# Batch 0's scores in six units instead of seven, and more turns by DMA, in a block-sparse attention and feed-forward kernel

## The chip, the cores and the metric

One core of one Trainium2 chip. The metric is the device time of one execution in microseconds (us). Where a time is given as a median, the lowest and highest run stand beside it at its first mention. The profile's span is about 1.7 us shorter than the time of the same run.

Engines by the profile's names: PE is TensorE, DVE is VectorE, ACT is ScalarE, POOL is GpSimd, SP is SyncE, whose queue issues the DMAs.

## The reference

Attention over 4 batches of 8 heads, 768 positions and 64 dimensions, then a feed-forward layer on the 3072 tokens. A query sees its own block of 64 keys and the three blocks that its gate scores highest, and no later key.

```python
k_rep = k.reshape(B, H, 12, 64, 64).mean(axis=3)            # one mean key per block
gate  = einsum('bhsd,bhnd->bhsn', q, k_rep)                 # later blocks set to -1e9
mask  = top-3 blocks of gate, plus the own block, and key position <= query position
attn  = softmax(where(mask, q @ k.T / 8, -1e9)) @ v
x     = attn.transpose(0, 2, 1, 3).reshape(3072, 512)
out   = gelu_tanh(x @ w_in) @ w_out                         # 512 -> 2048 -> 512
```

## The kernel before

Two heads make a "pair"; pair p belongs to batch p // 4 (HP = 4). Each batch passes three stages: its heads (four pairs), the first layer with gelu ("s1"), and the second layer ("s2"). A list scheduler in Python (`Plan.solve`) is given each piece of work with its engines, an assumed cost, its dependencies, a priority and, for a DMA, a `lag` until it lands. It fixes the order of every engine when the kernel is built; on the chip each engine works through its list and waits where an operand is late. Second-layer matmuls of the batch ahead fill PE where the heads leave room, and 110 filler matmuls on zeros of the lowest priority fill what planned gaps are left. Fillers that find no gap come at the end.

The block mask is a matrix of 12 rows per head. It is computed with queries on the partitions, turned, and added to the scores by a matmul. The normalised output `xn` must be turned too, to be the first layer's operand `xT`. The kernel has two ways for both: six (or five) PE transposes with a copy out of PSUM, or one transposing DMA from the SP queue.

```python
def by_xbar(p):                       # mask rows turned by DMA?
    return p >= 2 * HP
# ... in pre(p), the work ahead of a pair
if by_xbar(p):
    go = add({SP: 1.0}, mask_dma, [sel], pr - 20)          # dma_start_transpose
    m = add({"NONE": 0.0}, lambda _: None, [go], pr, lag=3.0)
else:
    m = add({PE: 0.31}, mask, [sel], pr, takes=("mk", ("mk", p)))
mcs = [add({DVE: 0.4, ACT: 0.6}, mc(h), [m, old.get("s")], pr)
       for h in ((None,) if early else (0, 1))]
# ... in turn(p, norms), the output of a pair of batches 1 to 3
if p >= HP + 2 and hp < HP - 1:
    go = add({SP: 1.0}, ot_dma, norms, base - 20)          # dma_start_transpose
    ...
    return
ot = add({PE: 0.36}, ot_e, norms, base + 50, takes=("pre", ("oT", p)))
```

Batch 0 is special: there is no second layer to fill PE with. Its pairs take both heads in one unit of scores. A unit holds a wide PSUM tile (two exist) from its score matmuls until its exp has read it; POOL then clears the upper triangle of a diagonal tile, and PE multiplies with the values.

```python
units = [[(0, 0, 384)], [(1, 128, 256), (2, 256, 128)], [(0, 384, 384)],   # (key tile, first query, width)
         [(1, 384, 384)], [(2, 384, 384)], [(3, 384, 384)],
         [(4, 512, 256), (5, 640, 128)]]
def both_heads(p):
    for ui, pieces in enumerate(units):
        st = add({PE: 0.45}, st_e, ..., takes=("wide", ("st",) + u))       # scores, then mask
        ex = add({ACT: 0.71}, ex_e, [st, ...], gives=[("st",) + u])        # exp, 128 x 768
        af = add({POOL: 0.36}, af_e, [ex], pr)                             # diagonal tiles only
        pvs.append(add({PE: 0.212}, pv_e, [af, ld["v16", p], ...]))        # times values
        # after units 1 and 6: DVE normalises a half, PE turns it
```

Loads, and the fillers:

```python
ld[key, p] = add({"NONE": 0.0}, lambda _: None, [go], prio=1000 * b + hp, lag=1.9)
...
def warm():
    for n in range(110):
        def emit(_, n=n):
            nc.tensor.matmul(plan.buf["warm", n][:, 0:256], zero, z, start=True, stop=True)
        add({PE: 0.107 if n > 26 else 0.214}, emit, [], 1e6, takes=("warm", ("warm", n)), gives=[("warm", n)])
```

Lines of the kernel that the profile names: L850 batch 0's scores, L868 their exp, L900 their value matmuls, L934 batch 0's output transposes, L977 those of later batches, L521 gates, L567 mask transposes, L587 mask turns by DMA, L984 output turns by DMA, L1018 first layer, L1031 gelu, L1052 second layer, L1089 fillers, L224 and L234 loads. From L850 on, the changed kernel has each one line later (L851, L869 and so on).

The softmax here doesn't subtract the row's maximum and nothing guards it: scores larger than these inputs give would overflow.

Of the kernel before, what the change touches and what calls it, by code (L numbers as in the profile page):

```python
# [9 lines left out]
FP16 = mybir.dt.float16  # L10
# [23 lines left out]
class Plan:  # L34
# [13 lines left out]
    def add(self, *a, **kw):  # L48
        op = Op(*a, **kw)
        self.ops.append(op)  # L50
        return op
# [70 lines left out]
def kernel(  # L122
# [16 lines left out]
    HP = H // 2  # L139
# [11 lines left out]
    iov = ctx.enter_context(tc.tile_pool(name="iov", bufs=PV))  # L151
    hd = ctx.enter_context(tc.tile_pool(name="hd", bufs=3))
    hd2 = ctx.enter_context(tc.tile_pool(name="hd2", bufs=2))
    atp = ctx.enter_context(tc.tile_pool(name="atp", bufs=7))
    xtp = ctx.enter_context(tc.tile_pool(name="xtp", bufs=2))
    gtp = ctx.enter_context(tc.tile_pool(name="gtp", bufs=2))
    obp = ctx.enter_context(tc.tile_pool(name="obp", bufs=3))
# [35 lines left out]
    PE, ACT, DVE, POOL, SP = "PE", "ACT", "DVE", "POOL", "SP"  # L193
    add = plan.add
    T = {}
# [10 lines left out]
        return p >= FIRST_DVE  # L206

    def by_xbar(p):
        return p >= 2 * HP


    SRC = {"k": k, "q": q, "v": v}
# [154 lines left out]
    rdy = {}  # L367
# [381 lines left out]
    def heads(p):  # L749
        b, hp = divmod(p, HP)  # L750
        i = p % NB
        base = 1000 * b + 100 * hp
        norms = []
        for h in range(2):
            pvs = []
            for gi, (ja, jb) in enumerate(groups):
                u = (p, h, gi)
                pr = base + 10 * (3 * h + gi)
                wa = S - ja * 128
                wb = S - jb * 128  # L760

                def st_e(_, u=u, ja=ja, jb=jb, wa=wa, wb=wb, h=h):
                    st = plan.buf[("st",) + u]
                    for jc, cb in ((ja, 0), (jb, wa)):
                        s0 = jc * 128
                        w = S - s0
                        x = cb
                        while x < cb + w:
                            e = min(cb + w, (x // 512 + 1) * 512)
                            k0, q0 = slice(s0, s0 + 128), slice(  # L770
                                s0 + (x - cb), s0 + (e - cb))
                            nc.tensor.matmul(  # L772
                                st[:, x:e], kT16[i][h][0:76, k0],
                                qT16[i][h][0:76, q0],
                                start=True, stop=True)
                            x = e
                st = add({PE: 0.381}, st_e, rdy[p][h], pr,
                         takes=("wide", ("st",) + u))

                def ex_e(_, u=u, n=wa + wb):  # L780
                    T["at", u] = atp.tile([128, 896], FP16, tag="at",
                                          name="at_%d_%d_%d" % u)
                    nc.scalar.activation(
                        out=T["at", u][:, 0:n],
                        in_=plan.buf[("st",) + u][:, 0:n],
                        func=AF.Exp, bias=0.0, scale=SCALE)
                ex = add({ACT: 0.8}, ex_e,
                         [st, table(("exp", b), gelus.get(b - 1, []), base)],
                         pr,
                         gives=[("st",) + u])  # L790
                exps.setdefault(b, []).append(ex)

                def af_e(_, u=u, wa=wa):
                    at = T["at", u]
                    dg = bass.AP(at.tensor, at.offset,
                                 [at.ap[0], [wa, 2], [1, 128]])
                    nc.gpsimd.affine_select(
                        out=dg, in_=dg, compare_op=ALU.is_ge, fill=0.0,
                        base=0, pattern=[[0, 2], [1, 128]],
                        channel_multiplier=-1)  # L800
                af = add({POOL: 0.36}, af_e, [ex], pr)

                def pv_e(_, u=u, ja=ja, jb=jb, wa=wa, h=h, gi=gi):
                    pvv = plan.buf["pv", p, h][:, 0:NC * 66].rearrange(
                        "p (c w) -> p c w", w=66)
                    at = T["at", u]
                    for jc, cb in ((ja, 0), (jb, wa)):
                        for qc in range(jc, NC):
                            nc.tensor.matmul(
                                pvv[:, qc, 0:65],  # L810
                                at[:, cb + (qc - jc) * 128:
                                   cb + (qc - jc + 1) * 128],
                                v16[i][:, jc, h, :],
                                start=(gi == 0 and jc == 0 and qc == 0),
                                stop=(gi == 2 and jc == jb and qc == NC - 1),
                                skip_group_check=True)
                pvs.append(add({PE: 0.212}, pv_e,
                               [af, ld["v16", p], c_E["ones", i]] + pvs[-1:],
                               pr, takes=("pv", ("pv", p, h))))

            norms.append(norm(p, h, pvs, base - 20))
        turn(p, norms)
        last.setdefault(p, {}).update({"s": st, "k": st, "v": pvs[-1]})


    units = [[(0, 0, 384)], [(1, 128, 256), (2, 256, 128)], [(0, 384, 384)],
             [(1, 384, 384)], [(2, 384, 384)], [(3, 384, 384)],
             [(4, 512, 256), (5, 640, 128)]]

    def both_heads(p):  # L830

        b, hp = divmod(p, HP)
# [3 lines left out]
        pvs = []  # L836
        for ui, pieces in enumerate(units):
            u = (p, ui)
            pr = base + 10 * ui

            def st_e(_, u=u, pieces=pieces):

                st = plan.buf[("st",) + u]
                for mask in range(2):
                    x = 0
                    for j, q0, w in pieces:
# [8 lines left out]
                                start=x == 0 and not mask, stop=bool(mask),  # L855
                                skip_group_check=True)
                        x += w
            st = add({PE: 0.45}, st_e, rdy[p][0 if ui < 2 else 1], pr,
                     takes=("wide", ("st",) + u))

            def both(t, lo, hi):
                return t[:, 0:768].rearrange("p (h w) -> p h w", h=2)[
                    :, :, lo:hi]

            def ex_e(_, u=u):
                T["at", u] = atp.tile([128, 896], FP16, tag="at",
                                      name="at_%d_%d" % u)
                nc.scalar.activation(  # L868
                    out=both(T["at", u], 0, 384),  # L869
                    in_=plan.buf[("st",) + u].rearrange(  # L870
                        "p (h w) -> p h w", h=2)[:, :, 0:384],
                    func=AF.Exp, bias=0.0, scale=SCALE)
            ex = add({ACT: 0.71}, ex_e,
                     [st, table(("exp", b), [], base)], pr,
                     gives=[("st",) + u])
            exps.setdefault(b, []).append(ex)
# [1 line left out]
            for n, (j, q0, w) in enumerate(pieces):  # L878
                if q0 != 128 * j:
                    continue  # L880
                x = sum(w for _, _, w in pieces[:n])

                def af_e(_, u=u, x=x):
                    dg = both(T["at", u], x, x + 128)
                    nc.gpsimd.affine_select(
                        out=dg, in_=dg, compare_op=ALU.is_ge, fill=0.0,
                        base=0, pattern=[[0, 2], [1, 128]],
                        channel_multiplier=-1)
                af = add({POOL: 0.36}, af_e, [ex], pr)

            half = 0 if ui < 2 else 1

            def pv_e(_, u=u, ui=ui, pieces=pieces, half=half):
                pvv = plan.buf["pv", p, half][:, 0:NC * 66].rearrange(
                    "p (h c w) -> p h c w", h=2, w=66)
                x = 0
                for j, q0, w in pieces:
                    for c in range(q0 // 128, (q0 + w) // 128):
                        for h in range(2):
                            nc.tensor.matmul(  # L900
                                pvv[:, h, c - 3 * half, 0:65],
                                both(T["at", u], x, x + 128)[:, h],
                                v16[i][:, j, h, :],
                                start=(ui in (0, 2) and x == 0 and h == 0),
                                stop=(ui in (1, len(units) - 1)
                                      and x == 256 and h == 1),
                                skip_group_check=True)
                        x += 128
            pvs.append(add({PE: 0.212}, pv_e,
                           [af, ld["v16", p], c_E["ones", i]] + pvs[-1:],  # L910
                           pr, takes=("pv", ("pv", p, half))))
            if ui == 1 or ui == len(units) - 1:
# [56 lines left out]
    def turn(p, norms):  # L969

        b, hp = divmod(p, HP)
# [13 lines left out]
                out=T["xT", b][:, hp, :].rearrange("p (c q) -> p c q", q=128),  # L985
                in_=T["xn", p].rearrange("p c h d -> p (c h d)"))

        if p >= HP + 2 and hp < HP - 1:
            go = add({SP: 1.0}, ot_dma, norms, base - 20)
            xts.setdefault(b, []).append(  # L990
                add({"NONE": 0.0}, lambda _: None, [go], base - 20,
                    lag=3.0))
            return
# [171 lines left out]
```

## Time and profile before

| | before |
|---|---|
| time | 275.11 us (275.07 to 275.27, 3 runs) |
| span of the profiled run | 273.8 us (that run took 275.51 us) |
| PE busy | 97% |
| first scores of batch 0 / last value matmul of batch 0 | 12.59 / 45.06 us |
| first scores of batch 1, 2, 3 | 66.64 / 132.56 / 193.15 us |

The page of the kernel before: the span, busy time of each engine, and the chain of work that ended last by engine.

```profile
span 273.8 us, 5919 instructions
PE 265.1 (97%) x2290; PEld 153.7 (56%) x2290; DVE 142.2 (52%) x468; ACT 187.4 (68%) x245; POOL 48.5 (18%) x112
PE 63%; DVE 12%; SPq 9%; DMA 6%; ACT 5%; issue 3%; POOL 0%; DVEq 0%; ACTq 0%
```

PE is busy for 97% of the span, but that counts the fillers. The mean hides stages with different limits. What PE waited for in the kernel before (in total, times, longest, in us):

```profile
PE bank_90 L977 <- DVE xn_1329 L964: 1.1, 1, 1.1
PE wide_89 L850 <- ACT at_0_468 L868: 0.8, 1, 0.8
PE bank_92 L977 <- DVE xn_2574 L964: 0.7, 1, 0.7
...
PE bank_90 L521 <- DVE ksb_108 L472: 0.4, 1, 0.4
PE bank_93 L521 <- DVE qT_6_1289 L422: 0.4, 1, 0.4
PE bank_93 L567 <- DVE madd_132 L548: 0.4, 1, 0.4
```

Apart from waits in the first 12 us, that is most of PE's idle time: 1.06 us before the output transposes of pair 4, 0.75 us before scores of batch 0 (for an exp on ScalarE), 0.70 us before the output transposes of pair 11, some 0.4 us before gates and mask transposes. Most are waits for VectorE. The busy time of each engine by window, in the kernel before (columns: window, its length, then busy us and instructions of PE, PE's weight loads, DVE, ACT, POOL, then clock, DMA share, GB/s), two windows of batch 0's heads:

```profile
20.00:28.00 8.00, 6.65 (x96) 3.74 (x94) 7.28 (x28) 5.94 (x9) 1.84 (x5) 1.00 0.89 132
28.00:36.00 8.00, 8.00 (x121) 4.66 (x121) 7.83 (x28) 7.32 (x11) 4.39 (x9) 1.00 1.07 156
```

and two of batch 1's heads:

```profile
70.00:86.00 16.00, 14.18 (x159) 8.19 (x157) 14.47 (x37) 14.52 (x19) 4.07 (x10) 1.00 0.79 143
86.00:102.00 16.00, 15.78 (x181) 8.96 (x180) 15.50 (x51) 15.21 (x19) 6.17 (x14) 1.00 1.00 161
```

In batch 1's heads VectorE is busy for 14.47 and 15.50 us of 16 while PE is the engine that should be the limit. PE's long waits for it, 0.40, 0.37 and 1.06 us, lie in the first of the two windows; in the second PE is idle for 0.22 us only. In batch 0's heads, from 28 us on, VectorE is at 7.83 of 8 and ScalarE at 7.32.

The durations of the exp in batch 0, from ScalarE's timeline of the kernel before (start, us, instruction):

```profile
36.69 0.81 ACT L868 ACTIVATE at_0_815<-wide_89 128x768 f16<-128x768 f32 x1
37.39 0.80 ACT L868 ACTIVATE at_1_830<-wide_88 128x768 f16<-128x768 f32 x1
```

And VectorE's timeline of the kernel before around the values of pair 3, the load that batch 0 uses last, and the queries of pair 4, the first pair of batch 1. A bracket at the end of such a line would give idle time just before it and what ended it; there is none:

```profile
31.73 0.55 DVE L203 CAST v_137<-v_sd_610 128x768 f16<-128x768 f32 x1
...
34.52 0.97 DVE L422 STREAM_TRANSPOSE qT_4_777<-q_sd_650 128x768 f32<-128x768 f32 x1
```

The 1.06 us wait ends with `xn_1329`, pair 4's output normalised on VectorE. It stood there behind work for pair 7 and a copy of mask rows:

```profile
79.08 0.96 DVE L422 STREAM_TRANSPOSE kT_7_1390<-k_sd_1261 128x768 f32<-128x768 f32 x1
80.42 0.48 DVE L203 COPY qT_0_127<-bank_93 12x640 f16<-12x640 f16 x1 [0.38 <-ACT qT_1_128 L199]
...
82.81 0.56 DVE L964 TENSOR_TENSOR xn_1329<-bank_90,zr_1_1436 128x384 f16<-128x384 f32 x1
```

### The profile page before, as it was taken

What the parts mean: (1) busy time and instruction counts of PE and PEld (TensorE: products, weight loads), DVE (VectorE), ACT (ScalarE), POOL (GpSimd) and SP (SyncE); (2) the same over time, 40 slices, a digit from 0 to 9 for tenths busy, and PEclk for the clock granted to TensorE, in tenths of its full rate; (3) what the DMA queues carried; (4) which work ended last, traced back from release to release, by engine and by line L of the source; (5) the groups of instructions that cost most, each with busy time, mean ns of one, the idle gap of its engine ahead of it and who ended that gap; (6) DMA issues with size and microseconds to landing.
All of it is one profiled execution on the core that took longest, in us unless ns stands there. A gap on an engine that the chain in (4) does not pass through costs nothing.

```text
span 273.8 us, 5919 instructions
## 1 busy us (share of the span) xinstructions
PE 265.1 (97%) x2290; PEld 153.7 (56%) x2290; DVE 142.2 (52%) x468; ACT 187.4 (68%) x245; POOL 48.5 (18%) x112
## 2 busy tenths in 40 slices
PE   8798999999998999999999989999999999999998
PEld 5664557665454554455566534565566545665447
DVE  6778997107899996857499968500133300000001
ACT  3477887757989994896999853766899713654110
POOL 5041633000122420000045500000154200000000
PEclk9999999999999999999999999999999999999999
DMA  5999999999889969989999963300022122000222
GB/s 127 229 186 138 139 203 189 190 186 152 123 161 166 156 132 195 220 128 176 163 178 173 148 132 102 86 2 0 0 69 63 36 79 77 0 2 0 77 77 79
DMA packets 133824, 32.44 MB, mean 118 GB/s; under 512 B 127524, under 2 KB 129828, under 8 KB 133796
## 3 DMA queue, kind: packets, MB, share of 16 engines
q1 hardware_dynamic: 130676, 27.87, 58.9%
q0 software_dynamic: 3120, 4.19, 9.2%
q8 instruction: 18, 0.29, 0.5%
q14 instruction: 10, 0.08, 0.1%
HBM read 27.26 MB, written 6.29 MB: 123 GB/s over the span
## 4 chain that ended last, share of the span: by engine, by line
PE 63%; DVE 12%; SPq 9%; DMA 6%; ACT 5%; issue 3%; POOL 0%; DVEq 0%; ACTq 0%
PE wide_89 L1018 13%; PE wide_88 L1018 12%; PE bank_90 L1052 7%; PE bank_93 L1052 6%; SPq L224 5%; PE bank_91 L1052 4%; PE bank_92 L1052 3%; SPq L234 3%; PE wide_89 L772 2%; PE wide_88 L772 2%; DMA v_sd_383<-in_v_dram 2%; DMA q_sd_1856<-in_q_dram 1%; DMA q_sd_2172<-in_q_dram 1%; SPq L245 1%; PE wide_88 L850 1%
## 5 line engine op out<-in xcount | busy, mean ns | idle before, releaser
L1018 PEld LDWEIGHTS <-w_in_113 128*128 128x128 f16 x512 | 49.7, 98 | 34.0 <-issue 1.1
L203 DVE COPY osb_5_3665<-bank_92 128x256 f32<-128x256 f32 x1 | 0.4, 424 | 49.7 <-PE bank_92 L1052 49.7
L1052 PEld LDWEIGHTS <-gT_3416 128*128 128x128 f16 x112 | 11.0, 98 | 9.9
L1089 PEld LDWEIGHTS <-zero 128*128 128x128 f16 x110 | 10.4, 104 | 6.0 <-issue 3.0
L1052 PEld LDWEIGHTS <-gT_2805 128*128 128x128 f16 x96 | 9.1, 97 | 8.1
L1052 PEld LDWEIGHTS <-gT_1921 128*128 128x128 f16 x96 | 8.8, 97 | 8.5 <-issue 0.8
L1052 PE MATMUL bank_90<-w_out_114,gT_1921 128*128 128x512 f16 x48 | 13.3, 380 | 0.0
L1052 PEld LDWEIGHTS <-gT_1015 128*128 128x128 f16 x96 | 8.6, 98 | 7.3 <-issue 0.3
L1052 PE MATMUL bank_93<-w_out_114,gT_1015 128*128 128x512 f16 x48 | 12.6, 379 | 0.0
L1018 PE MATMUL wide_89<-xT_1468,w_in_113 128*128 128x512 f16 x64 | 12.1, 326 | 0.1
L1018 PE MATMUL wide_88<-xT_3083,w_in_113 128*128 128x512 f16 x64 | 12.0, 326 | 0.0
L1018 PE MATMUL wide_88<-xT_422,w_in_113 128*128 128x512 f16 x64 | 11.9, 326 | 0.0
L1018 PE MATMUL wide_89<-xT_422,w_in_113 128*128 128x512 f16 x64 | 11.9, 326 | 0.0
L1018 PE MATMUL wide_88<-xT_1468,w_in_113 128*128 128x512 f16 x64 | 11.9, 326 | 0.0
L1018 PE MATMUL wide_88<-xT_2372,w_in_113 128*128 128x512 f16 x64 | 11.7, 326 | 0.0
L1018 PE MATMUL wide_89<-xT_3083,w_in_113 128*128 128x512 f16 x64 | 11.7, 326 | 0.0
L1018 PE MATMUL wide_89<-xT_2372,w_in_113 128*128 128x512 f16 x64 | 11.7, 326 | 0.0
L203 DVE COPY osb_0_2977<-bank_93 128x512 f32<-128x512 f32 x1 | 0.7, 691 | 19.9 <-PE bank_93 L1052 19.9
L742 ACT ACT_TABLE_LOAD x8 | 10.3, 1283 | 0.9 <-PEq L1149 0.8
L1089 PE MATMUL bank_93<-zero 128*128 128x256 f16 x33 | 9.2, 287 | 0.7 <-ACT kT_0_123 L199 0.7
L1052 PE MATMUL bank_91<-w_out_114,gT_2805 128*128 128x512 f16 x32 | 9.7, 379 | 0.0
L1031 ACT ACTIVATE gT_2805<-wide_88 128x768 f16<-128x768 f32 x8 | 6.5, 812 | 4.2 <-PE wide_88 L1018 4.1
(954 smaller groups left out, 661.6 us busy)
## 6 DMA issues: line engine op xcount, KB each, us to landing
w_in_113<-in_moe_w_in_dram POOLq DMA_DIRECT2D x2, 1024.0 KB, 11.7
w_out_114<-in_moe_w_out_dram POOLq DMA_DIRECT2D x1, 2048.0 KB, 16.6
k_sd_139<-in_k_dram SPq DMA_DIRECT2D x4, 96.0 KB, 2.4
q_sd_140<-in_q_dram SPq DMA_DIRECT2D x4, 96.0 KB, 2.4
k_sd_209<-in_k_dram SPq DMA_DIRECT2D x2, 192.0 KB, 3.9
q_sd_225<-in_q_dram SPq DMA_DIRECT2D x2, 192.0 KB, 4.4
v_sd_249<-in_v_dram SPq DMA_DIRECT2D x2, 192.0 KB, 4.4
k_sd_276<-in_k_dram SPq DMA_DIRECT2D x2, 192.0 KB, 4.5
```

The lines of the kernel that those rows point to most:

```text
L203: nc.vector.tensor_copy(out=out, in_=in_)
L224: nc.sync.dma_start(out=sd[:, :, hh, :], in_=SRC[key][b, 2 * hp + hh].rearrange("(c p) d -> p c d", p=128))
L234: nc.sync.dma_start(out=sd[64 * hh + 32 * a:64 * hh + 32 * a + 32], in_=SRC[key][b, 2 * hp + hh].rearrange("(t i) (a j) -> a i t j", i=32, ...
L245: nc.sync.dma_start(out=sd[:, 3 * a:3 * a + 3, hh, :], in_=SRC[key][b, 2 * hp + hh].rearrange("(a c p) d -> a p c d", p=128, c=3)[a])
L742: nc.scalar.activation(out=t, in_=bmask[:, 0, 0:1], func=AF.Exp if key[0] == "exp" else AF.Gelu_apprx_tanh, bias=0.0, scale=1.0)
L772: nc.tensor.matmul(st[:, x:e], kT16[i][h][0:76, k0], qT16[i][h][0:76, q0], start=True, stop=True)
L850: nc.tensor.matmul(st[:, 512 * h + x + lo - q0:512 * h + x + w], (T["E2"][h] if mask else kT16[i][0])[r, j * 128:(j + 1) * 128], qT16[i][m ...
L1018: nc.tensor.matmul(hps[:, u:e], w_in16[:, ci, f * 128:(f + 1) * 128], T["xT", b][:, ci, u:e], start=(ci == 0), stop=(ci == HP - 1))
L1031: nc.scalar.activation(out=T["gT", b][:, f, :], in_=plan.buf["hps", b, f][:, 0:S], func=AF.Gelu_apprx_tanh, bias=0.0, scale=1.0)
L1052: nc.tensor.matmul(plan.buf["ops", b, n][:, 0:x1 - x0], T["gT", b][:, f, ti * 128:(ti + 1) * 128], w_out16[:, f, x0:x1], start=(f == 0), s ...
L1089: nc.tensor.matmul(plan.buf["warm", n][:, 0:256], zero, z, start=True, stop=True)
```

## The change

Its intent: fewer hand-overs per pair in batch 0, and PE, VectorE and ScalarE relieved in batch 1's heads, at the price of six more DMA transposes on the SP queue.

```diff
     def by_xbar(p):
-        return p >= 2 * HP
+        return p >= HP
...
-    units = [[(0, 0, 384)], [(1, 128, 256), (2, 256, 128)], [(0, 384, 384)],
-             [(1, 384, 384)], [(2, 384, 384)], [(3, 384, 384)],
-             [(4, 512, 256), (5, 640, 128)]]
+    units = [[(0, 0, 384)], [(1, 128, 256), (2, 256, 128)],
+             [(0, 384, 384), (4, 512, 128)], [(1, 384, 384), (4, 640, 128)],
+             [(2, 384, 384), (5, 640, 128)], [(3, 384, 384)]]
...
-            st = add({PE: 0.45}, st_e, ...
+            st = add({PE: 0.43 if W == 384 else 0.55}, st_e, ...      # W: width of the unit
-            ex = add({ACT: 0.71}, ex_e,
+            ex = add({ACT: 0.71 if W == 384 else 0.9}, ex_e,
-            pvs.append(add({PE: 0.212}, pv_e,
+            pvs.append(add({PE: 0.212 if W == 384 else 0.28}, pv_e,
...
-        if p >= HP + 2 and hp < HP - 1:
+        if p >= HP and hp < HP - 1:
```

(The tiles of the exp's result grow from 896 to 1024 columns and their pool shrinks from 7 to 6.) Output turns of pairs 4 and 5 are new to the DMA; pair 6's went by DMA already. The costs in `add` are what the planner assumes, so the change alters the static order of all engines too.

More of the change, by code (lines that the diff above doesn't have):

```diff
@@ L153 @@
     hd2 = ctx.enter_context(tc.tile_pool(name="hd2", bufs=2))
-    atp = ctx.enter_context(tc.tile_pool(name="atp", bufs=7))
+    atp = ctx.enter_context(tc.tile_pool(name="atp", bufs=6))
     xtp = ctx.enter_context(tc.tile_pool(name="xtp", bufs=2))
@@ L780, in ex_e @@
                 def ex_e(_, u=u, n=wa + wb):
-                    T["at", u] = atp.tile([128, 896], FP16, tag="at",
+                    T["at", u] = atp.tile([128, 1024], FP16, tag="at",
                                           name="at_%d_%d_%d" % u)
@@ L839, in both_heads @@
             pr = base + 10 * ui
+            W = sum(w for _, _, w in pieces)
             def st_e(_, u=u, pieces=pieces):
@@ L857, in st_e, with both, ex_e @@
                         x += w
-            st = add({PE: 0.45}, st_e, rdy[p][0 if ui < 2 else 1], pr,
+            st = add({PE: 0.43 if W == 384 else 0.55}, st_e, rdy[p][0 if ui < 2 else 1], pr,
                      takes=("wide", ("st",) + u))
-            def both(t, lo, hi):
-                return t[:, 0:768].rearrange("p (h w) -> p h w", h=2)[
+            def both(t, lo, hi, W=W):
+                return t[:, 0:2 * W].rearrange("p (h w) -> p h w", h=2)[
                     :, :, lo:hi]
-            def ex_e(_, u=u):
-                T["at", u] = atp.tile([128, 896], FP16, tag="at",
+            def ex_e(_, u=u, W=W, both=both):
+                T["at", u] = atp.tile([128, 1024], FP16, tag="at",
                                       name="at_%d_%d" % u)
                 nc.scalar.activation(
-                    out=both(T["at", u], 0, 384),
+                    out=both(T["at", u], 0, W),
                     in_=plan.buf[("st",) + u].rearrange(
-                        "p (h w) -> p h w", h=2)[:, :, 0:384],
+                        "p (h w) -> p h w", h=2)[:, :, 0:W],
                     func=AF.Exp, bias=0.0, scale=SCALE)
-            ex = add({ACT: 0.71}, ex_e,
+            ex = add({ACT: 0.71 if W == 384 else 0.9}, ex_e,
                      [st, table(("exp", b), [], base)], pr,
@@ L881, in both_heads, with af_e @@
                 x = sum(w for _, _, w in pieces[:n])
-                def af_e(_, u=u, x=x):
+                def af_e(_, u=u, x=x, both=both):
                     dg = both(T["at", u], x, x + 128)
@@ L891, in both_heads, with pv_e @@
             half = 0 if ui < 2 else 1
-            def pv_e(_, u=u, ui=ui, pieces=pieces, half=half):
+            def pv_e(_, u=u, ui=ui, pieces=pieces, half=half, W=W, both=both):
                 pvv = plan.buf["pv", p, half][:, 0:NC * 66].rearrange(
@@ L905, in pv_e @@
                                 stop=(ui in (1, len(units) - 1)
-                                      and x == 256 and h == 1),
+                                      and x == W - 128 and h == 1),
                                 skip_group_check=True)
                         x += 128
-            pvs.append(add({PE: 0.212}, pv_e,
+            pvs.append(add({PE: 0.212 if W == 384 else 0.28}, pv_e,
                            [af, ld["v16", p], c_E["ones", i]] + pvs[-1:],
```

## The prediction

> **What bounds it.** The page shows PE busy 97%, but that includes 110 filler matmuls on zeros. The windows by source line split the run. In 12.6-44 us (batch 0's heads) PE is not the limit: about 40 fillers fit there, while ScalarE is about 85% busy. Each score unit is a ring over two wide PSUM tiles: scores, exp, diagonal mask on POOL, value matmuls. From 44 us on PE is the limit, nearly without idle time, except in batch 1's heads (66.6-113 us), where the wait view shows 2.5 us of PE idle: 1.06 us before the output transpose of pair 4, 0.40 before a gate, 0.37 before mask transposes, 0.41 before another gate. ScalarE and VectorE are 90-97% busy in 70-100 us.
>
> **What changes.**
> 1. Batch 0: 24 score units instead of 28, same columns. Exps of 768 columns start 0.71 us apart, those of 896 about 0.81, so 1024 takes about 0.92 (estimate). ScalarE saves only 4x0.71 - 12x0.21 = 0.3 us; the Trainium skill, "ScalarE: Activation LUTs" (What ACT_TABLE_LOAD costs), says 0.833 ns per element and an overlap back to back, and the trace agrees (0.81 us for 768, 0.91 for 896). The larger part is one hand-over round less per pair (0.1-0.3 us idle per unit) and one mask instead of two in series (0.41 us each) after a pair's last exp. I expect batch 0's heads to end 1.0-1.8 us earlier.
> 2. PE loses the mask transposes of pairs 4-7 (about 0.29 us each) and output transposes of pairs 4 and 5 (0.35 us each): 1.9 us, of which 1.6 lies where PE is the limit. Pair 6's went by DMA already. Two copies of 128x768 (ACT 0.80, DVE 0.56) vanish; mask copies from SBUF take DVE 0.32 instead of 0.48.
> 3. The sync queue gets six DMA transposes, 1.2-1.4 us of issue each and about 3 us to landing in the trace: some 7.5 us more on a queue that was about 80% occupied in 62-113 us. In order: a transpose that waits holds back later loads.
> 4. Order: the second matmul of batch 0 (96 matmuls) is now used up inside batch 1's heads, where 35 were left for afterwards; 9 fillers stand before batch 1's first matmul. 17 fillers now stand in the middle (4 before), +1.4 us; 11 leave the tail, where the chain runs through them: about -0.4 us.
>
> **Sum.** Batch 0 -1.3; PE work -1.6; fillers +1.4; tail -0.4; idle of batch 1's heads between -2 and +1.5, taken as -0.5. Total -2.4.
>
> **Prediction: 272.6 us, 270.2 to 275.4.** Faster by over 2%: 0.10; within 2%: 0.88; slower: 0.02.
>
> **What would show it.** Batch 0's last value matmul ends at 43-44 us instead of 45.0 and first-layer matmuls start 1-2 us earlier; the 1.06 and 0.37 us waits are gone; second-layer matmuls between batch 1's heads and its first layer are gone, with fillers there; exp of 1024 columns 1.02 us. Batches 2 and 3 take the same time.
>
> **What would make it wrong.** Batch 0 bound by loads and VectorE rather than by score units (no gain there). Pair 5's keys land at 61 us whatever batch 0 does: then its gate waits. The sync queue saturated: late mask rows stop PE at pairs 5-7, late keys and queries at the gates of pairs 8-10; then about 275 or more. If VectorE's and ScalarE's relief removes most of batch 1's idle time: 270.

## The result and the profile after

271.17 us (270.86 to 271.86, 6 runs) against 275.00 us (274.83 to 275.27, 6 runs) of the kernel before. The ratio is 0.9866, 95% interval 0.9851 to 0.9881. Ratios here are the mean time of one kernel's fast runs over that of the other's of the same rounds, so not quite the ratio of the medians quoted. The change is faster by 1.3%, which is within the 2% that counts as the same; the prediction's range holds it.

The page of the changed kernel, the same lines:

```profile
span 269.5 us, 5885 instructions
PE 262.6 (97%) x2274; PEld 153.2 (57%) x2274; DVE 141.3 (52%) x466; ACT 185.4 (69%) x241; POOL 48.4 (18%) x112
PE 58%; SPq 14%; DMA 11%; DVE 11%; issue 3%; ACT 2%; DVEq 0%; POOL 0%; ACTq 0%
```

PE lost 2.5 us of busy time, but the span lost 4.3 (the medians differ by 3.8; the profiled run of the kernel before took 275.51 us, above the six timed beside the changed kernel, and 0.45 us of the 4.3 lie before the first scores). What PE waited for in the changed kernel, the largest after the first 12 us:

```profile
PE bank_93 L521 <- DVE qT_2_454 L203: 0.4, 1, 0.4
PE bank_90 L521 <- DVE qT_6_1331 L422: 0.3, 1, 0.3
PE wide_89 L1019 <- ACT gT_1857 L1032: 0.3, 1, 0.3
PE bank_92 L901 <- POOL at_5_445 L886: 0.3, 1, 0.3
```

The long waits for VectorE's `xn` (1.1 and 0.7 us) and for `madd_132` are gone. Batch 1's heads in the changed kernel:

```profile
70.00:86.00 16.00, 15.56 (x158) 8.40 (x157) 14.13 (x49) 13.96 (x18) 4.73 (x12) 1.00 1.11 171
86.00:102.00 16.00, 16.00 (x146) 8.56 (x144) 12.25 (x34) 13.33 (x17) 4.46 (x10) 1.00 0.97 196
```

In the second window VectorE is busy 12.25 us of 16 where it was 15.50. But the waits that went lay in the first, where VectorE's busy time fell only from 14.47 to 14.13. So a lower load on VectorE is not what the windows show as the cause. Its timeline shows another candidate: `xn` of pair 4 now stands before pair 7's keys.

```profile
80.30 0.56 DVE L965 TENSOR_TENSOR xn_1317<-bank_93,zr_1_1401 128x384 f16<-128x384 f32 x1
81.98 0.98 DVE L422 STREAM_TRANSPOSE kT_7_1439<-k_sd_1344 128x768 f32<-128x768 f32 x1 [1.12 <-DMA k_sd_1344<-in_k_dram]
```

Batch 0's heads in the changed kernel:

```profile
20.00:28.00 8.00, 7.14 (x120) 4.61 (x122) 7.61 (x29) 4.94 (x7) 2.62 (x6) 1.00 0.85 133
28.00:36.00 8.00, 7.52 (x116) 4.75 (x113) 7.15 (x26) 5.80 (x8) 4.18 (x8) 1.00 1.07 156
```

ScalarE, which the units were meant to serve better, now sits idle for 2.2 us of the 8 from 28 us on. Its timeline in the changed kernel shows the 1024-column exp, and one of the reasons for that idle time:

```profile
35.94 0.83 ACT L199 CAST qT_0_115<-qT_4_787 64x768 f16<-64x768 f32 x1 [1.77 <-DVE qT_4_787 L422]
...
39.08 1.02 ACT L869 ACTIVATE at_2_867<-wide_88 128x1024 f16<-128x1024 f32 x1
40.00 1.02 ACT L869 ACTIVATE at_3_882<-wide_89 128x1024 f16<-128x1024 f32 x1
```

VectorE's timeline in the changed kernel, at the same two instructions as before:

```profile
31.25 0.56 DVE L203 CAST v_137<-v_sd_628 128x768 f16<-128x768 f32 x1 [0.27 <-DMA v_sd_628<-in_v_dram]
...
34.93 0.98 DVE L422 STREAM_TRANSPOSE qT_4_787<-q_sd_662 128x768 f32<-128x768 f32 x1 [0.41 <-DMA q_sd_662<-in_q_dram]
```

Now VectorE waits for loads, and ScalarE waits 1.77 us for VectorE. The queue of SP in the changed kernel (start, us of issue):

```profile
47.05 15.16 SPq L234 DMA_DIRECT2D k_sd_1121<-in_k_dram  x4
...
79.86 1.25 SPq L587 DMA_TRANSPOSE mT_1411<-madd_132  x1
81.15 2.27 SPq L234 DMA_DIRECT2D q_sd_1430<-in_q_dram  x4
83.53 1.22 SPq L985 DMA_TRANSPOSE xT_1486<-xn_1317  x1
```

Pair 5's keys took 15 us to issue (9 us before; the trace does not say why), but its keys and queries together took 17.4 us instead of 19.1, and PE shows no wait for them.

To see where the time came from I summed PE's timeline by stage. Each matmul is charged the time from its start to the next one's start, less the idle time that the profile states; a stage runs from a batch's first score matmul to the next batch's. One profiled execution of each kernel, in us:

| stage | before | after | what moved most |
|---|---|---|---|
| until batch 0's first scores | 12.59 | 12.14 | when the first loads land; no part of the change |
| batch 0 | 54.05 | 53.88 | mask transposes −0.45, scores −0.52, idle +0.92 |
| batch 1 | 65.92 | 64.14 | idle −1.62, mask transposes −0.91, output transposes −0.69, fillers +1.24, second layer +0.77 |
| batch 2 | 60.59 | 59.16 | second layer −1.56, idle −0.55, fillers +0.44 |
| batch 3, to the last second-layer matmul | 76.57 | 76.79 | |
| from there to the end | 4.08 | 3.39 | 16 fillers instead of 27 |

"Second layer" fell in batch 2 since the changed order places five of these matmuls (0.22 us each) elsewhere, four in batch 1's stage and one in batch 3's. Over the batches: idle −1.25, mask transposes −1.36, output transposes −0.88, scores −0.95, fillers +1.35. Idle time and fillers are both PE time without real work, and together they did not fall (+0.10): where PE waited before, it now runs more fillers. So the 4.3 us are nearly all in four pieces: transposes −2.24, scores −0.95, the end −0.69 and the start −0.45.

### The profile page after: what moved, and what is told of

Its sections match the earlier page's. It is cut to its first block, busy times and chain, and to the rows that moved or that the text cites. A ratio compares the mean times of both kernels' runs of the same rounds, so it can differ in the third digit from the quotient of the medians.

```text
span 269.5 us, 5885 instructions
## 1 busy us (share of the span) xinstructions
PE 262.6 (97%) x2274; PEld 153.2 (57%) x2274; DVE 141.3 (52%) x466; ACT 185.4 (69%) x241; POOL 48.4 (18%) x112
## 4 chain that ended last, share of the span: by engine, by line
PE 58%; SPq 14%; DMA 11%; DVE 11%; issue 3%; ACT 2%; DVEq 0%; POOL 0%; ACTq 0%
PE wide_88 L1019 11%; PE wide_89 L1019 10%; PE bank_93 L1053 6%; SPq L234 6%; PE bank_90 L1053 6%; PE bank_92 L1053 6%; SPq L224 5%; PE bank_91 L1053 5%; PE wide_89 L772 3%; PE wide_88 L772 3%; DMA v_sd_390<-in_v_dram 2%; DMA v_sd_1201<-in_v_dram 2%; DMA q_sd_662<-in_q_dram 2%; DMA k_sd_2216<-in_k_dram 1%; SPq L245 1%
## 5 line engine op out<-in xcount | busy, mean ns | idle before, releaser
L1090 PEld LDWEIGHTS <-zero 128*128 128x128 f16 x110 | 11.1, 106 | 5.0 <-issue 1.4
L1053 PE MATMUL bank_92<-w_out_114,gT_1857 128*128 128x512 f16 x48 | 13.2, 380 | 0.0
L1019 PE MATMUL wide_88<-xT_1486,w_in_113 128*128 128x512 f16 x64 | 12.2, 326 | 0.2 <-ACT gT_1857 L1032 0.2
L1019 PE MATMUL wide_88<-xT_3077,w_in_113 128*128 128x512 f16 x64 | 12.2, 326 | 0.0
L1019 PE MATMUL wide_89<-xT_1486,w_in_113 128*128 128x512 f16 x64 | 11.9, 326 | 0.3 <-ACT gT_1857 L1032 0.3
L1019 PE MATMUL wide_88<-xT_431,w_in_113 128*128 128x512 f16 x64 | 12.0, 326 | 0.0
L1019 PE MATMUL wide_88<-xT_2337,w_in_113 128*128 128x512 f16 x64 | 11.9, 326 | 0.0
L1019 PE MATMUL wide_89<-xT_431,w_in_113 128*128 128x512 f16 x64 | 11.9, 326 | 0.0
L1019 PE MATMUL wide_89<-xT_3077,w_in_113 128*128 128x512 f16 x64 | 11.7, 326 | 0.0
L1019 PE MATMUL wide_89<-xT_2337,w_in_113 128*128 128x512 f16 x64 | 11.7, 326 | 0.0
L1090 PE MATMUL bank_93<-zero 128*128 128x256 f16 x33 | 9.2, 286 | 0.7 <-ACT kT_0_123 L199 0.7
L1053 PE MATMUL bank_90<-w_out_114,gT_2771 128*128 128x512 f16 x32 | 9.7, 380 | 0.0
L1053 PE MATMUL bank_91<-w_out_114,gT_1857 128*128 128x512 f16 x32 | 9.7, 379 | 0.0
L1090 PE MATMUL bank_90<-zero 128*128 128x256 f16 x29 | 8.5, 292 | 1.2 <-DVE bmask L170 1.1
```

The costliest lines, as they stand in the source:

```text
L1019: nc.tensor.matmul(hps[:, u:e], w_in16[:, ci, f * 128:(f + 1) * 128], T["xT", b][:, ci, u:e], start=(ci == 0), stop=(ci == HP - 1))
L1053: nc.tensor.matmul(plan.buf["ops", b, n][:, 0:x1 - x0], T["gT", b][:, f, ti * 128:(ti + 1) * 128], w_out16[:, f, x0:x1], start=(f == 0), s ...
```

## The experiments

Twelve runs were made in four sets (e5 is the kernel of e1 again), each set on one chip beside runs of the kernel before (medians 274.99 to 275.23 us). All gave correct results. A fourth buffer for the values, tried as a way to load them earlier, did not build: 6 kB per partition were wanted for the last pool and 3.3 were left.

The theory from the prediction: each part saves what it takes off PE or off the ring of score units, so the parts add. Rivals: the gain comes from the relief of VectorE and ScalarE (their late results made PE wait), or from the static order that the planner happens to find.

### One part at a time

The units alone are the changed kernel with both conditions restored:

```diff
 def by_xbar(p):
-    return p >= HP
+    return p >= 2 * HP
...
-        if p >= HP and hp < HP - 1:
+        if p >= HP + 2 and hp < HP - 1:
```

> The new score units alone (transposes as before). Theory A, from the two traces: batch 0's heads are not bound by the hand-over of units, and the gain lies in batches 1 and 2; then this gives 0 to -0.8 us (274.2 to 275.0 us), with the end of batch 0's last value matmul less than 0.6 us earlier. Rival B, the prediction on record: -1.0 to -1.8 us from batch 0, so 273.2 to 274.0. In this build 30 fillers stand in the tail (27 before), which by the chain of waits costs about 0.3 us in either theory.

Both DMA parts alone are the kernel before with these two conditions changed the other way round.

> The DMA transposes alone (28 score units as before). Theory A: -2.8 to -3.6 us (271.4 to 272.2), nearly all of the change. Rival B: PE work -1.6, fillers +1, tail -0.4, idle -0.5: about -1.0 to -2.0 us (273.0 to 274.0). Theory C, that the new static order and not the parts made the gain: the two parts do not add up to -3.8 us, by more than 1 us.

The mask rows alone, `by_xbar` changed in the kernel before:

> Only the mask rows of pairs 4 to 7 by DMA. Theory A: PE loses 15 transposes in batch 1 (0.91 us in the trace) and the 0.37 us wait for madd; the 1.06 us wait before the output transpose of pair 4 stays. About -1.0 to -1.8 us. 16 fillers stand in the middle in this order. Rival (sync queue): in-order DMA issue holds loads back, and it gives 0 or is slower.

The outputs alone, the other condition changed in the kernel before:

> Only the outputs of pairs 4 and 5 by DMA. Theory A: PE loses 12 transposes (0.69 us), and the waits of 1.06 and 0.70 us before output transposes: -1.0 to -2.2 us. Rival B (work only): -0.7 us. Together with the mask part it should give the DMA part within 0.7 us if the parts add.

Measured, in one set of 5 rounds beside the kernel before at 275.16 us (274.74 to 277.34, 11 runs):

| kernel | median (lowest to highest) us | ratio [95%] |
|---|---|---|
| units alone (e1) | 277.45 (275.86 to 278.05) | 1.0067 [1.0035, 1.01] |
| both DMA parts (e2) | 272.74 (272.49 to 274.73) | 0.9917 [0.9886, 0.9949] |
| mask rows alone (e3) | 274.37 (273.64 to 275.49) | 0.9968 [0.994, 0.9997] |
| outputs alone (e4) | 275.75 (274.76 to 276.54) | 1.0015 [0.9984, 1.0046] |
| all parts | 271.17, another set | 0.9866 [0.9851, 0.9881] |

No time lies in a range that a theory named for it: the units alone and the outputs alone were expected to gain and did not, and the other two fell between their theories. Only theory C of e2, that the parts would not add, held. Units +0.67%, mask rows −0.32% and outputs +0.15% would make +0.5%; the whole change made −1.34%. The units lose 0.67% alone, and yet they take the DMA version from 0.9917 to 0.9866. So the first theory falls as a sum, though its PE terms are real: the stage table of e2 shows mask transposes at 1.03 us instead of 2.23 and output transposes at 2.69 instead of 3.39.

PE's idle time in batch 1 falls from 2.46 to 0.52 us in e2 (in batch 2 it rises from 0.70 to 1.33), and its fillers there take 0.76 us, hardly more than the 0.60 before. With the mask rows alone (e3) idle time is 0.63 us, and neither the 1.06 nor the 0.37 us wait is left; but fillers take 2.21 us there, and the stage is only 0.14 us shorter. With the outputs alone (e4) batch 1's idle time rises to 3.41 us. The 1.06 us wait did not go with the transposes that had it. A second-layer matmul waits in their place for the same `xn`, which also frees its PSUM bank:

```profile
82.89 0.59 PE L1052 MATMUL bank<-w_out,gT 128*128 128x512 f16 x2 [1.05 <-DVE xn L964]
```

So the mask rows took that wait away, though in e3 mostly in exchange for fillers. How is not separated: in e3, as in the changed kernel, `xn` stands before pair 7's keys in VectorE's list, in e4 behind them as in the kernel before. This place is the planner's; the relief of VectorE and ScalarE as such, in one and the same order, was not tested.

Where did the units lose? In e1's trace not in batch 0: counted from its first scores, the last value matmul ends after 31.0 us instead of 32.5. What PE waited for in e1:

```profile
PE bank L1053 <- DVE xn L965: 2.0, 1, 2.0
PE bank L521 <- DVE qT L422: 1.2, 2, 0.9
```

Batch 1's stage is 1.0 us longer than before and batch 2's idle time is 2.00 us instead of 0.70: the time was lost in stages whose work the units do not touch. But the execution traced took 275.86 us, only 0.35 us more than the traced one of the kernel before; it does not show the whole loss of 2.3 us.

### The same kernel again

e1's profiled run was the fastest of its runs, 275.86 us beside a median of 277.45. (Two of the six were at a clock of 0.994, 278.01 and 278.05 us; the four at 1.0 spread from 275.86 to 277.67.)

> The new score units alone, once more, for a second trace: five of six timed runs of it lay at 276.4 to 278.1 us, and the traced one at 275.9. Theory D: a load that lands later in those runs stops the in-order PE at a gate or at an output transpose, so a trace of a slow run shows one or two more PE waits of 0.5 to 2 us that end with a VectorE instruction behind a key or query load. Rival E: the whole run is slower by small amounts, with no wait that stands out.

Measured: 277.29 us, one run. The 2.0 us wait is there too, so it belongs to the order and not to one execution. In addition there is a wait in batch 0 that e1's trace lacks. VectorE's timeline of e1,

```profile
30.92 0.72 DVE L203 CAST v<-v_sd 128x768 f16<-128x768 f32 x1
```

and of e5, the same instruction:

```profile
31.77 0.73 DVE L203 CAST v<-v_sd 128x768 f16<-128x768 f32 x1 [0.76 <-DMA v_sd<-in_v_dram]
```

The values of pair 3 landed later, `xn` came later, and PE stood 0.9 us before the output transposes at 33.8 us. That is theory D but for the load, which is one of values. Same kernel, same order, 1.4 us more. Here batch 0's stage is 0.57 us longer than in the kernel before and batch 1's 1.71, so this slower execution loses in batch 0 too: its last value matmul ends 32.3 us after the first scores. It is the first hint at what limits batch 0 once the units are fewer. That this load explains the whole spread of e1's runs isn't shown: only two of them have a trace.

### Only the order moved

To tell the units' work from their order, one constant of the planner changed in e1's kernel. The instructions stay the same.

```diff
-                         prio=1000 * b + hp, lag=1.9)
+                         prio=1000 * b + hp, lag=2.6 if p >= HP else 1.9)
```

> The new score units alone, with one constant of the planner changed: loads of pairs 4 and up are assumed to land 2.6 us after their issue and not 1.9. No instruction is added or removed; only the static order moves (32 second-layer matmuls of batch 0 stay behind batch 1's heads, as in the kernel before). Theory D (the loss of the units alone is one of order): 274.0 to 275.2, at least 2 us below the units alone. Rival: the units themselves cost the time, then it stays at 276.5 to 278.

Measured: 274.19 us (274.05 to 274.65), ratio 0.9961 [0.9943, 0.9979]. That is 3.3 us faster than e1 with the same instructions, and the 2.0 us wait has become 0.9. What was still possible is that this constant gives any version a better order. So it was put into the kernel before:

> The kernel before with the one constant of e6: the planner is told that loads of pairs 4 and later land 2.6 us after their issue instead of 1.9; same instructions, another static order (second-layer matmuls of batch 0: 63 in batch 1's heads and 32 after, 5 fillers there, tail 27 fillers, as in the kernel before nearly). Theory D (the constant mended an order that only the units alone had got wrong; the kernel before's order was good already): 274.2 to 276.0, ratio 0.997 to 1.003. Theory G (2.6 us is closer to the true landing time and gives any version a better order, so that e6 says nothing of the units): 272.5 to 273.5, ratio 0.990 to 0.994. With e6 at 274.19, the units alone under the mended constant are worth the difference: D about -1, G about +1 us.

Measured: 275.69 us (275.50 to 276.24), ratio 1.0026 [1.0014, 1.0038]. The kernel before gets slightly worse. The constant is no general gain; e1's order was bad. With it, the units are worth 274.19 against 275.69, −1.5 us (by the ratios −1.8); on top of the DMA parts, 271.17 against 272.74, they are worth −1.6 us (by the ratios −1.4; different sets both). So the units are worth about −1.5 us in two settings, and +2.3 in the third, that of e1. Each of these is the units together with the order that comes with them.

The same constant in the changed kernel, as a candidate for a better version:

> The changed kernel with the same constant of 2.6 us: same instructions, another order; 96 second-layer matmuls of batch 0 in batch 1's heads as in the changed kernel, 4 fillers in the middle instead of 17, tail 16, but 21 fillers instead of 15 inside batch 0's first layer. Theory F (the 17 fillers in the middle only fill waits, as e8's 0.5 us said): 270.4 to 271.6, ratio 0.982 to 0.987. Theory G (a better order for any version): 268.5 to 270.3, ratio below 0.982. If the order gets worse as it did for the units alone: over 272.

Measured: 271.85 us (270.77 to 273.27), ratio 0.9879 [0.9853, 0.9905]. No gain, and a little outside the range of every theory: batch 1's stage is 1.3 us shorter with fewer fillers in the middle (8 instead of 17 in all; the expectation miscounted them as 4), but six fillers more stand in batch 0's first layer and PE waits 0.88 us there for a gelu, so batch 0's stage is 1.05 us longer. PE's time on fillers is 8.88 us over the stages, as in the changed kernel (8.86).

### Fillers

The prediction charged +1.4 us for 13 fillers more in the middle and −0.4 us for those that left the end. Two kernels left fillers out of the emission, without touching the plan: those from the 84th on in the kernel before (its last 27), and the 17 in the middle of the changed kernel.

```diff
             def emit(_, n=n):
+                if n >= 83:                 # in e8: if 77 <= n < 94:
+                    return
```

> The kernel before, without the 27 filler matmuls after the last real one; nothing else differs. Theory from the chains of waits: the end follows the fillers, and without them the last store; -0.5 to -0.8 us (274.3). Rival: the last store bounds the end in both, 0.

Measured: 274.94 us (274.30 to 277.10), ratio 1.0000 [0.9969, 1.0031]; the clock of its profiled run is 0.994. The medians differ by 0.25 us. This is unclear. The two runs at a clock of 1.0 took 274.30 and 274.47 us, and in the traced execution the stretch after the last second-layer matmul is 0.46 us shorter (3.62 instead of 4.08) while the first scores came 1.09 us later, at 13.68 us. That leans to the expected 0.5 us, but the runs as a whole do not show it.

> The changed kernel without the 17 fillers that stand in batches 1 and 2 (the 9 before the first layer of batch 1 among them); order otherwise the same. The prediction charged them 1.4 us. If PE time they take is real, 269.8 us; rival: they only fill waits that PE would have anyhow, then the waits appear as idle time and it stays within 0.3 us of 271.2.

Measured: 270.71 us (269.91 to 272.07), ratio 0.9840 [0.9811, 0.9869], beside 0.9866 for the changed kernel in another set. That is −0.5 us by the medians and −0.7 by the ratios, between the two expectations, and the intervals overlap. In its trace, batch 1 spends 1.84 us less on fillers, but PE waits 1.12 us for a gelu, a wait that was 0.3 us at most with the fillers in place, and its stage is only 0.63 us shorter:

```profile
PE wide L1019 <- ACT gT L1032: 1.1, 1, 1.1
```

Over batches 1 and 2 the fillers gave up 2.28 us, of which 0.47 show as a shorter stage; 0.91 came back as idle time, and the rest as more time charged to other matmuls. So in this execution most of a middle filler's time was no loss, and charging it in full as work was wrong.

### What holds batch 0

Batch 0 was to end 1.0 to 1.8 us sooner; counted from its first scores, the last value matmul ends after 32.09 us instead of 32.47. Counted from the span's start it ends at 44.23 us instead of 45.06, 0.83 us sooner, of which 0.45 is the earlier start. Which count is right is open: in e7, with batch 0 as in the kernel before, the first scores came 1.09 us later and the last value matmul still ended at 45.05. The units took less time from PE and ScalarE, but idle time grew by 0.92 us. The suspicion from e5 and from VectorE's timeline: loads and VectorE. In the plan, the keys of pair 4 (of batch 1) are issued before the values of pair 3. One dependency puts them behind:

```diff
                 for key in "kq":
-                    load(HP, key, None)
+                    load(HP, key, went["v", p])
```

> The changed kernel, but the loads of pair 4's keys and queries are issued after the values of pair 3, which VectorE waits for in batch 0 (0.27 us in the changed kernel, 0.76 us in the second run of the units alone). Theory L (batch 0 gained next to nothing because loads and VectorE bind it, as the prediction had it among its ways to be wrong): VectorE's wait for the values of pair 3 is gone, the last value matmul of batch 0 ends 0.3 to 0.9 us sooner counted from the first scores (32.1 us in the changed kernel), and the time is 270.2 to 270.9. Theory S (score units bind it): VectorE's wait is gone too, but the value matmuls end within 0.2 us of 32.1; the time is 271.0 to 271.6. Later keys of pair 4 could make its gate wait; then more than 271.6.

Measured: 271.43 us (271.00 to 272.70), ratio 0.9878 [0.9858, 0.9899]. VectorE waits for no load between 20 us and the end of batch 0's heads, and the last value matmul ends 30.73 us after the first scores, 1.36 us sooner than in the changed kernel. That speaks for theory L, but the total lies in the range of theory S. And e11 changed two things, as its trace shows: the planner gave the cast of these values to ScalarE, so VectorE had less work as well.

```profile
28.13 0.83 ACT L199 CAST v<-v_sd 128x768 f16<-128x768 f32 x1 [1.09 <-DMA v_sd<-in_v_dram]
```

The last kernel keeps that cast on VectorE:

```diff
         free_sd["v", p] = ld["v16", p] = add(
-            {DVE: 0.47, ACT: 0.8}, emit,
+            {DVE: 0.47} if p == HP - 1 else {DVE: 0.47, ACT: 0.8}, emit,
```

> As e11, but the cast of pair 3's values stays on VectorE (e11's planner had given it to ScalarE, so e11 both landed the values earlier and took 0.56 us off VectorE; one line allows VectorE alone for this cast). 62 fillers stand in batch 0's heads, as in the changed kernel. Theory L1 (the late landing of the values is what took batch 0's gain): VectorE does not wait for them, and the last value matmul ends 30.6 to 31.2 us after the first scores, as in e11 (30.7). Theory L2 (VectorE's amount of work is what binds): no wait for them either, but 31.5 to 32.1 us, as in the changed kernel (32.1). Time: L1 270.5 to 271.5, L2 271.2 to 272.2; the second run of batch 1's heads is where e11 lost its gain again (batch 1's stage 65.0 us instead of 64.1).

Measured: 271.64 us (271.19 to 272.25, 4 runs), ratio 0.9868 [0.9848, 0.9889]. VectorE's timeline of e12 has the cast without a wait:

```profile
30.81 0.76 DVE L203 CAST v<-v_sd 128x768 f16<-128x768 f32 x1
```

The last value matmul ends after 31.40 us, between the two expectations; the total lies in the range of L2. Of the 1.36 us, 0.69 came with the earlier landing alone, and 0.67 with the cast off VectorE. Counted from the span's start, it is 0.73 and 0.33 us. So both may have a share, but neither share is shown. These are single executions, and two executions of one kernel, e1 and e5, differ by 1.29 us in this measure (31.04 and 32.33). An order can do as much, too: in e9, with the old units, the value matmuls end after 31.39 us, although that batch's stage as a whole is 54.42 us, longer than before.

Neither e11 nor e12 is faster in total than the changed kernel. In e11, of the 1.35 us that batch 0's stage gained (52.53 after 53.88), batch 1's stage gave back 0.85 (64.99 after 64.14), with a new wait of 0.72 us for POOL. No version that ran beats the changed kernel beyond the intervals; e8 is the nearest.

## Why the prediction was right or wrong

The total was right: 272.6 predicted, 271.17 measured. The terms, against the profiled runs:

| term | predicted | shown |
|---|---|---|
| batch 0 | −1.3 us | −0.17 (its stage), −0.38 (to the last value matmul), −0.83 (the same from the span's start) |
| PE work | −1.9 in all, −1.6 where it counts | −2.24 in all, −1.60 in batch 1 |
| fillers in the middle | +1.4 | +1.68 on PE; taking them out gained about 0.5 to 0.7, not clear of the noise |
| tail | −0.4 | −0.69 |
| idle of batch 1's heads | −0.5 | −1.62 for the stage |
| batch 2 | 0 | −1.43 |

- **Right: the PE work.** It is the largest piece of the gain. The mask and output transposes went, and with them 2.05 us; the other 0.19 of the 2.24 is batch 0's output transposes, which stayed. The 1.06 and 0.37 us waits are gone, and so are the second-layer matmuls of batch 0 between batch 1's heads and its first layer; fillers stand there.
- **Right: the exp.** A 1024-column exp takes 1.02 us and the next starts 0.92 us later. The Trainium skill, "ScalarE: Activation LUTs" (What ACT_TABLE_LOAD costs), gives 186 ns plus 0.833 ns per element with an overlap of about 93 ns between neighbours: by estimate 1.04 and 0.95 us for 1024. The trace agrees within 0.03 us.
- **Mis-sized: batch 0.** "I expect batch 0's heads to end 1.0-1.8 us earlier" took the ring of score units as the limit. In its own terms, the last value matmul was to end at 43 to 44 us and ended at 44.23. PE's scores in batch 0 did take 0.52 us less and ScalarE was less busy, but PE's idle time there grew by 0.92 us, among others in waits for VectorE, which itself waited 0.27 and 0.41 us for loads. The prediction had this among its ways to be wrong. What could have warned: VectorE busy for 7.83 us of 8 from 28 us on, with no wait for loads. That VectorE and the loads are the limit fits e5, e11 and e12 but is not proved by them.
- **Mis-sized: idle time.** "Idle of batch 1's heads between -2 and +1.5, taken as -0.5." Most of the 1.62 us became fillers (+1.24); the two together fell by 0.38 us in batch 1, where the sum had them at +0.9 for the middle. The six new transposes on SP did not hold up PE, and the 1.06 and 0.37 us waits went with the mask rows (e3 against e4). The size fits the prediction's own alternative, 270 if the relief of VectorE and ScalarE removes most of batch 1's idle time; but that the relief did it, and not the place of `xn` in the new order, isn't shown.
- **Wrong: "Batches 2 and 3 take the same time."** Batch 3 does, within 0.22 us. Batch 2 is 1.43 us shorter: five second-layer matmuls moved to other stages, four of them to batch 1's, and the wait for pair 11's output, 0.70 us, nearly went. Batch 2's own heads and layers do the same work, so this is order.
- **Wrong in kind: the fillers.** They were charged at PE's time. In e8's trace, 2.28 us less of them made the stages only 0.47 us shorter.
- **Not asked: do the parts add?** The prediction summed them. The single parts sum to a loss, and their union is the best of all. The errors above partly cancelled in the sum (batch 0 too good by 1.1 us, idle time and batch 2 too bad by 2.5 together), so the close total is in part luck and not proof of the reasoning.

What stays open: why the planner's order of the units alone leaves a 2.0 us wait is shown only as far as that a constant that moves nothing but the order takes 3.3 us off. The 2.0 us wait fell to 0.9; which placement costs the rest was not isolated. Open, too, is how the mask rows by DMA took away batch 1's waits, and what limits batch 0.

## What to carry to other kernels

Where a scheduler fixes the order of all engines, a change is a new order as well as new work: test a part under two orders before calling it a gain or a loss, since here one part was worth +2.3 us in one setting and about −1.5 us in two others. When one resource is shortened, look for the engine that is nearly always busy beside it and for the loads behind that engine. Count fillers together with idle time (here idle fell by 1.25 us and fillers grew by 1.35), and before a filler is charged at its full time, take it out and see what the stages gain (here 0.47 us for 2.28). And when a wait is to be removed, look at where the late result stands in its engine's list: the 1.06 us wait passed to the next instruction when only the one that had waited was taken away.

## What the Trainium skill lacked or had wrong

- "Advanced Engine Details and Errata" (X-Bar Transpose (TRN2)) says that transposing DMAs are as fast as ordinary ones. For landing, most of what is here agrees: 2.6 to 4.6 us from issue in the changed kernel (3.5 for pair 4's output turn), beside 3.8 us (median) for the loads of pair 3's values. The one exception is pair 4's mask rows, 8.6 us, at a time when loads of keys took 4.6 to 15.6 us as well. What it and "DMA: Bandwidth & Descriptors" (DMA Transpose (X-bar)) lack is a time in microseconds that one such transpose of this size, from SBUF to SBUF, occupies the issuing queue: here 1.2 to 1.4 us, twice 2.3, which is what a static plan must budget.
- "DMA: Bandwidth & Descriptors" (Issuing engines are not separate DMA queues) calls the time on the sequencer usually small relative to the DMA itself. In these traces it adds up: the four DMAs that load pair 7's queries took 2.27 us of issue on SP in the changed kernel, some 0.57 us each, beside 2.3 to 4.1 us (medians) from issue to landing of one for the loads of this form in its first 40 us.
- No page that I read warns that the order of a static plan moves the time as much as the work does: 277.45 and 274.19 us with the same instructions (e1 and e6).
